# Gated linear attention into a mixture of experts: row products over 128 rows of the array, empty rows written later, eight unread products fewer

## The chip, the cores and the metric

The kernel runs on one core of a Trainium2 chip. A core has engines that run side by side and meet only at semaphores: TensorE (PE in the profile; its weight loads are PEld), VectorE (DVE), ScalarE (ACT), GpSimd (POOL) and SyncE (SP), which here issues most of the transfers. TensorE multiplies out of on-chip memory (SBUF) into eight accumulation banks (PSUM). The metric is the device time of one execution in microseconds; the median of several runs is compared.

## The reference

Inputs q, k, v and a complex gate a are 4 batches x 8 heads x 768 steps x 48 channels, f32. First a gated recurrence runs over the steps of each head; then every token (3072 of them, 384 channels) goes to the one of eight experts with the highest logit:

```python
scale = np.minimum(mag, 0.999) / (mag + 1e-06)
for t in range(S):
    new_re = ar * S_re - ai * S_im
    new_im = ar * S_im + ai * S_re
    S_re, S_im = (new_re + kv, new_im)
    y[:, :, t] = np.einsum('bhd,bhde->bhe', q[:, :, t], S_re)
...
logits = x @ w_gate + modality_bias[modality_id]
e_idx = np.argmax(logits, axis=1)
h = np.maximum(x[mask] @ w1[e], 0.0)
out[mask] = gate_w[mask, None] * (h @ w2[e])
```

## The kernel before

The sequence is cut into 6 chunks of 128 steps; a chunk of one batch is a **unit**, so there are 24 units, taken in pairs (groups). Within a chunk the recurrence is written as a masked product. Logarithms of the moduli and turns of the phases are summed over the steps by TensorE (`sums`, L240; `angles`, L194), and ScalarE makes exponentials, sines and cosines of them. `hats` multiplies these into q and k (L276, L280). `turned` transposes the result (L304) with 64 rows of the array at a time. `inner` makes the masked weights (`wp`, L321) and the update of the state (`up`, L329). `outer` makes the unit's output y, transposed (`yp`, L353 and L359), in a tile whose partitions 0 to 63 and 64 to 127 hold an even and an odd head, 48 channels and 16 of zeros each; ScalarE copies it to `yT` (L360).

`rows` (L363) then turns y back into rows of tokens and makes the logits in the same products: the moving operand `sel` has an identity of 48 columns and the 48 x 8 gate weights behind it. One product per head: 4 pairs x 2 halves, each with 64 rows of the array and 56 columns, the two halves into two PSUM banks. ScalarE copies the 384 channels to bf16 (L381), and VectorE adds the eight partial logits per expert (L382).

The **router** (`take`, called after units 7, 15, 19 and 23) adds the bias, finds the best expert, ranks the tokens of each expert with small products (`rank`), and GpSimd scatters the rows to their expert's region in device memory (`x_rows`, L657). Unused places there are filled from two columns of 128 empty rows that the router's constructor writes once (L540). The constructor is called at the end of loop turn 0 and also loads the modality bias and the modality of each token (L555, L557), from which VectorE makes the bias of each token (L573 to L577).

The **expert layers** gather 256 rows at a time, transpose them (L922), multiply by w1 (L940), apply the ReLU, multiply by w2 (L955), scale by the gate weight (L958) and scatter to the output (L960).

`dense(to, n)` (L88) issues n products whose result nobody reads; they lie ahead of the transposes of certain units (`FILLED`, by unit number) and ahead of the `rank` products from unit 16 on (four, and none at the last take). Each carries an order edge to lie behind the last products traced before.

The loop at L434 traces one turn per unit, with every stage at its own offset: in turn w come the loads, `turned` of unit w+2, `sums` (even turns), `inner` of w+1, `outer` of w, `rows` of w-1, `angles` (odd turns to 15). The order in which each engine gets its instructions isn't that of the text throughout: a planner sets it at build time, from priorities, its own costs of instructions, and the times at which it expects operands, except where order edges or a hand-written stretch (the late expert layers) fix it. On each engine the order is then strict. The transfers of SP's queue also go out in that order, and one that waits holds up those behind it.

Of the kernel before, what the change touches and what calls it, by code (L numbers as in the profile page):

```python
# [11 lines left out]
F32 = mybir.dt.float32  # L12
BF16 = mybir.dt.bfloat16
AX = mybir.AxisListType
Alu = mybir.AluOpType
# [8 lines left out]
def gate_loop(nc, ctx, tc, cpool, ident, q, k, v, a_re, a_im, sel, lg, make_router, make_layers):  # L24
# [4 lines left out]
    B, H, S, D = q.shape  # L29
    L = 128  # L30
    G = S // L
    J = H // 2
    C = 2 * D
# [32 lines left out]
    box = {}  # L66
# [28 lines left out]
            if i == 0 and busy:  # L95
                tc.add_manual_dep(ins.ins, busy[-1].ins.name, mybir.DependencyInfo(mybir.DependencyClass.NoSync, mybir.DependencyReason.DATA), reason="behind the products before it")

    FILLED = {2: 10, 3: 5, 4: 5, 5: 5, 15: 4}

    abs_ = io.tile([L, 2, 2, NG, H, D], F32, name="abs", bufs=1)  # L100
    css = el.tile([L, 2, NG, H, 2, D], F32, name="css", bufs=1)
# [261 lines left out]
    def rows(g, b):  # L363

        yT = box.pop(("outer", g, b))
        xw = pair([L, J, D + Router.E], "xw")
        for j in range(J):
            for u in range(2):
                at_u = slice(u * 64, (u + 1) * 64)
                ins = nc.tensor.matmul(xw[:, u, j], yT[at_u, j], sel[at_u, j], start=True, stop=True)  # L370
        busy.append(ins)
        m = g * B + b
        m0 = max(c for c in takes.values() if c <= m)
        if m == m0:
            n = min([c for c in takes.values() if c > m] + [NU]) - m
            packed = un.tile([L, 8, Router.W], U32, name="packed")
            nc.gpsimd.iota(packed[:, 0:n, Router.W - 1].rearrange("p (g b) -> p g b", b=B), pattern=[[L, n // B], [S, B]], base=g * L, channel_multiplier=1)
            box["packed"] = packed
        packed = box["packed"]
        xr = packed[:, m - m0, 0:H * D // 2].bitcast(BF16)  # L380
        nc.scalar.copy(xr.rearrange("t (j u d) -> t u j d", u=2, d=D), xw[:, :, :, 0:D])  # L381
        nc.vector.tensor_reduce(lg[:, m, :], xw[:, :, :, D:].rearrange("t u j e -> t e u j"), axis=AX.XY, op=Alu.add)  # L382

    NX = len(groups)
    NU = len(order)
# [1 line left out]
    late = []  # L387
    EARLY = Router.EARLY
    takes = {7: 0, EARLY - 1: 8, 19: EARLY, NU - 1: 20}
# [42 lines left out]
    rt = None  # L432
    open_ = []
    for w in range(-4, NU + 1):  # L434


        even = w % 2 == 0
        x = w // 2

        n = w + 1 if w < 0 else w  # L440
        unit(values, n + 2)
        unit(values, n + 3)
        if even:
            phase(load_a, x + 6)
            phase(carries, x + 4)
            phase(fractions, x + 3)
        else:
            phase(load_qk, x + 3)
            phase(decays, x + 2)
            hats(n + 3)  # L450
            if w == -3:
                hats(0)
        unit(turned, n + 2)
        if even:
            if x + 2 < NX:
                table(EXP)
            phase(sums, x + 2)
            phase(moduli, x + 2)
            phase(logs, x + 4)
        elif x + 3 < NX:  # L460
            table(TRIG)
            phase(arctans, x + 4)
        unit(inner, n + 1)
        if even:
            for f in late:
                f(act)
            late.clear()
        unit(outer, n)
        if even:
            hats(n + 3)  # L470
            phase(tangents, x + 4)
        else:
            phase(waves, x + 3)
            phase(squares, x + 5)
            phase(products, x + 5)
        if w == NU:
            layers.turn(0)
        unit(rows, n - 1)
        if not even:
            phase(angles, x + 4)  # L480
        if w == 0:
            rt = make_router(ctx, ps, bank)
        open_ = [t for t in open_ if next(t, True) is None]
        if w - 1 in takes:
            open_.append(rt.take(takes[w - 1], w, late, box["packed"], lambda n: dense(box["full"][:, 0], n)))
            next(open_[-1])
        if w == 15:
            layers = make_layers(rt, io, el, un, bank, pair, abs_, css)
        if w > 15:
            layers.before(w, box)  # L490
# [5 lines left out]
class Router:  # L496
# [20 lines left out]
    def __init__(self, nc, ctx, tc, keep, ps, bank, lg, x_rows, moe_modality_id, moe_modality_bias, N, Dt, E, B, G):  # L517
# [19 lines left out]
        nc.gpsimd.memset(empty[:, 0:self.W - 1], 0)  # L537
        nc.gpsimd.memset(empty[:, self.W - 1:], self.FAR)
        self.blank = x_rows[E * self.S:E * self.S + 2 * TP, :]
        nc.sync.dma_start(out=self.blank[None], in_=empty[:, None, :].broadcast_to([1, 2 * TP, self.W]))  # L540
        self.expert = keep.tile([1, self.NE + self.NR + self.NSMALL + 1], I32, name="expert")
        self.column = keep.tile([1, self.NE + self.NR + self.NSMALL + 1], I32, name="column")
        self.SURE = self.NBIG + 1
# [41 lines left out]
            self.tc.declare_no_dep(put.ins, group="first loads", reason="the first tiles hold tokens of the first columns alone")  # L585
            self.tc.add_to_no_dep_group("late rows", put.ins)

    def take(self, m0, m1, late, packed, dense):

        nc, rp, TP, E = self.nc, self.rp, self.TP, self.E  # L590
        n = m1 - m0
        last = m1 == len(self.tile_of)
        M = 8

        def t(name, shape, dt=F32):
            full = rp.tile([TP, M] + shape, dt, name=name)
            return full[:, 0:n]

        def bc(ap):
            return ap[:, :, None].broadcast_to([TP, n, E])  # L600

        l = t("l", [E])
        nc.vector.tensor_tensor(l, self.lg[:, m0:m1], self.bias[:, m0:m1], Alu.add)
        mx = t("mx", [])
        nc.vector.tensor_reduce(mx, l, axis=AX.X, op=Alu.max)
        sh = t("sh", [E])
        nc.vector.tensor_tensor(sh, l, bc(mx), Alu.subtract)

        cand = t("cand", [E])
        nc.vector.scalar_tensor_tensor(cand, sh, 0.0, self.pref[:, None, :].broadcast_to([TP, n, E]), Alu.is_ge, Alu.mult)  # L610
        best = t("best", [])
        nc.vector.tensor_reduce(best, cand, axis=AX.X, op=Alu.max)
        oneh = t("oneh", [E], BF16)
        nc.vector.tensor_tensor(oneh, cand, bc(best), Alu.is_equal)
        before = self.acc
        acc = rp.tile([TP, E], BF16, name="acc", bufs=4)
        with nc.allow_low_precision("counts of at most 24"):
            nc.vector.tensor_reduce(acc[:], oneh.rearrange("p i e -> p e i"), axis=AX.X, op=Alu.add)
        if before is not None:
            nc.vector.tensor_tensor(acc[:], acc[:], before, Alu.add)  # L620
        self.acc = acc[:]

        def weights(act):
            ex = t("ex", [E])
            act(ex, sh, Act.Exp)
            sm = t("sm", [])
            nc.vector.tensor_reduce(sm, ex, axis=AX.X, op=Alu.add)
            nc.vector.reciprocal(packed[:, 0:n, self.W - 2].bitcast(F32), sm)

        late.append(weights)  # L630
        yield

        rank = self.bank([TP, M, E], "rank")
        if m0 >= self.EARLY:
            dense(0 if last else 4)
        nc.tensor.matmul(rank[:, 0:n], self.tri[:], oneh, start=True, stop=False)
        if before is not None:
            nc.tensor.matmul(rank[:, 0:n], self.ones[:], before[:, None, :].broadcast_to([TP, n, E]), start=False, stop=False)
        for i in range(n - 1):
            nc.tensor.matmul(rank[:, i + 1:n], self.ones[:], oneh[:, i:i + 1, :].broadcast_to([TP, n - 1 - i, E]), start=False, stop=i == n - 2)  # L640
        own = t("own", [E])
        nc.vector.tensor_tensor(own, rank[:, 0:n], oneh, Alu.mult)
        pos = t("pos", [])
        nc.vector.tensor_reduce(pos, own, axis=AX.X, op=Alu.add)
        nc.vector.scalar_tensor_tensor(pos, best, -float(self.S), pos, Alu.mult, Alu.add)
        place = t("place", [], U32)
        nc.vector.tensor_scalar(place, pos, float(E * self.S), None, Alu.add)
        if m0 == 0:
            self.guess()
        if m1 == self.EARLY:  # L650
            self.early_places()
        if not last:
            yield
        for i in range(n):
            if i == 4:
                yield
            put = self.put = nc.gpsimd.indirect_dma_start(out=self.x_rows, out_offset=bass.IndirectOffsetOnAxis(ap=place[:, i:i + 1], axis=0), in_=packed[:, i], in_offset=None, bounds_check=E * self.S - 1, oob_is_err=False)  # L657
            self.put_row(put, m0 >= self.EARLY)
        if m0 == self.EARLY:
            self.tc.add_manual_dep(nc.gpsimd.drain().ins, put.ins.name, mybir.DependencyInfo(mybir.DependencyClass.NoSync, mybir.DependencyReason.DATA), reason="the queue's list is cleared behind these")  # L660
        if last:
            self.places()
# [341 lines left out]
def kernel(  # L1004
# [27 lines left out]
    nc.vector.tensor_copy(identb[:], ident[:])  # L1032
    lg = cpool.tile([128, N // 128, E], F32, name="lg")

    sel = cpool.tile([128, H // 2, D + E], F32, name="sel")
    nc.gpsimd.memset(sel[:], 0.0)
    for u in range(2):
        nc.gpsimd.tensor_copy(sel[u * 64:u * 64 + D, :, 0:D], ident[u * 64:u * 64 + D, None, u * 64:u * 64 + D].broadcast_to([D, H // 2, D]))
        nc.sync.dma_start(out=sel[u * 64:u * 64 + D, :, D:], in_=moe_w_gate.rearrange("(j u d) e -> u d j e", u=2, d=D)[u])

    last, layers = gate_loop(
        nc, ctx, tc, cpool, ident, q, k, v, a_re, a_im, sel, lg,
# [33 lines left out]
```

## Time and profile before

| | us |
|---|---|
| median of three runs | 333.67 (334.74, 333.67, 328.97) |
| the profiled execution | 329.75 |
| its span in the profile | 328.1 |
| TensorE products / weight loads busy | 294.4 / 227.9 |
| VectorE busy | 242.2 |
| ScalarE busy | 240.5 |
| GpSimd busy | 70.2 |

The mean clock that TensorE was granted over the span is 0.969 of full speed. A row of instructions in order of time has its start, its length, the engine, the source line, the operation, the tiles (written<-read), the shapes (for a product rows*columns of the loaded operand and rows x columns of the moving one) and how many are merged; in brackets stand the engine's idle time before it and what ended that. A group's row has busy time and mean length in ns of one after the bar. Idle time of an engine that others don't wait for costs nothing.

### The profile page before, as it was taken

The page shows a single profiled execution, that of the slowest core. Times are in us where ns is not written, and L with a number is a line of the kernel's source. Part 1 is how long each engine was busy: PE and PEld are TensorE (multiplying, and loading weights), DVE is VectorE, ACT ScalarE, POOL GpSimd, SP SyncE. Part 2 cuts the span into 40 slices and gives each one's busy share as a digit, 9 for nine tenths or more (in the row PEclk, how much of TensorE's full clock was granted, in tenths as well). Part 3 has the DMA queues.
Part 4 walks back from the last instruction along what each step waited for, and adds up shares of the span by engine and source line. Part 5 has one row for each costly group of instructions (what it writes and reads, how often), then busy time and mean ns, then how long its engine had stood idle before and what let it go on. Part 6 is the DMA issues. An engine that isn't in the chain of part 4 may idle for free.

```text
span 328.1 us, 11561 instructions
## 1 busy us (share of the span) xinstructions
PE 294.4 (90%) x4950; PEld 227.9 (69%) x4950; DVE 242.2 (74%) x443; ACT 240.5 (73%) x289; POOL 70.2 (21%) x91
## 2 busy tenths in 40 slices
PE   1797899899499899989999999999998999999991
PEld 0343566658378686867778877889987677777770
DVE  1749699994679999999899987995436944555530
ACT  3889699999559899988999997655324666554541
POOL 8000000000000000001872000018541564332423
PEclk9899799979969999999999999999999999999998
DMA  7967897789884978676558977211591564332211
GB/s 135 208 139 147 168 193 125 114 79 176 177 170 89 160 168 154 140 142 135 132 118 141 190 131 147 51 28 54 100 231 59 152 212 147 98 119 97 100 62 57
DMA packets 155282, 43.04 MB, mean 131 GB/s; under 512 B 145602, under 2 KB 151494, under 8 KB 155096
## 3 DMA queue, kind: packets, MB, share of 16 engines
q1 hardware_dynamic: 149592, 31.98, 50.7%
q0 software_dynamic: 5632, 10.25, 11.7%
q8 instruction: 41, 0.67, 0.8%
q14 instruction: 17, 0.14, 0.1%
HBM read 38.00 MB, written 9.15 MB: 144 GB/s over the span
## 4 chain that ended last, share of the span: by engine, by line
PE 48%; ACT 26%; DVE 13%; issue 5%; DMA 4%; SPq 2%; POOL 1%; POOLq 0%; DVEq 0%; ACTq 0%
PE h_ps L940 9%; PE y_ps L955 9%; ACT sq L119 5%; ACT L116 5%; PE up L329 5%; PE xw L370 4%; PE ls L240 4%; PE yp L359 3%; ACT css L119 3%; ACT pm L119 3%; PE wp L321 3%; PE u L194 3%; PE yp L353 2%; DVE QK L280 2%; ACT KT L305 2%
## 5 line engine op out<-in xcount | busy, mean ns | idle before, releaser
L657 POOL DMA_INDIRECT x_rows<-packed,place x24 | 34.5, 1436 | 208.1 <-DVE lm L175 146.7
L280 DVE TENSOR_TENSOR QK<-css,qkp 128x1536 f32<-128x1536 f32 x24 | 42.0, 1751 | 0.1
L329 PE MATMUL up<-V,QK 64*96 64x48 f32 x704 | 37.5, 247 | 0.9 <-DVE lg L382 0.8
L329 PEld LDWEIGHTS up<-V,QK 64*96 64x96 f32 x704 | 34.5, 161 | 2.8 <-DVE lg L382 1.0
L955 PE MATMUL y_ps<-w2t,hT 128*128 128x384 bf16 x200 | 34.7, 326 | 0.7 <-ACT hT L943 0.7
L940 PE MATMUL h_ps<-xgT,w1t 128*128 128x256 bf16 (+1 forms) x312 | 34.9, 268 | 0.0
L116 ACT ACT_TABLE_LOAD x25 | 32.1, 1283 | 1.4 <-PEq L1060 0.9
L960 POOL DMA_INDIRECT out_dram<-y_sb,xg x25 | 25.4, 1014 | 35.8 <-ACT y_sb L958 31.5
L940 PEld LDWEIGHTS <-w1t 128*128 128x128 bf16 x312 | 29.5, 98 | 4.6
L305 ACT COPY KT<-tKT 96x1024 f32<-96x1024 f32 x24 | 24.2, 1008 | 9.0 <-PE tKT L304 8.8
L321 PEld LDWEIGHTS wp<-QT,KT 96*64 96x64 f32 x768 | 24.7, 139 | 8.6 <-ACT yT L360 2.8
L321 PE MATMUL wp<-QT,KT 96*64 96x64 f32 x768 | 28.0, 226 | 1.9 <-ACT yT L360 1.8
L958 ACT ACTIVATE y_sb<-y_ps,xg 128x384 f32<-128x384 f32 x25 | 13.2, 578 | 22.3 <-PE y_ps L955 18.2
L360 ACT COPY yT<-yp 128x512 f32<-128x512 f32 x24 | 14.0, 584 | 20.5 <-PE yp L359 20.3
L955 PEld LDWEIGHTS <-hT 128*128 128x128 bf16 x200 | 18.9, 98 | 12.5 <-issue 0.5
L370 PE MATMUL xw<-sel,yT 64*128 64x56 f32 x384 | 26.4, 277 | 0.6 <-ACT QT L305 0.6
L370 PEld LDWEIGHTS xw<-sel,yT 64*128 64x128 f32 x384 | 23.3, 187 | 2.6 <-ACT QT L305 0.7
L305 ACT COPY QT<-tQT 96x1024 f32<-96x1024 f32 x24 | 24.3, 1014 | 0.0
L119 ACT ACTIVATE sq<-sq 128x1536 f32<-128x1536 f32 (+1 forms) x20 | 23.3, 1165 | 1.4 <-DVE sq L150 1.2
L304 PEld LDWEIGHTS tKT<-ident,QK 64*96 64x96 f32 x384 | 13.2, 129 | 14.1 <-issue 8.2
L945 DVE TENSOR_SCALAR hT<-h_ps 128x1024 bf16<-128x1024 f32 (+1 forms) x9 | 10.5, 1166 | 16.8 <-PE h_ps L940 16.8
L119 ACT ACTIVATE pm<-ls 128x768 f32<-128x768 f32 x24 | 18.2, 809 | 6.5 <-PE ls L241 6.4
(197 smaller groups left out, 590.9 us busy)
## 6 DMA issues: line engine op xcount, KB each, us to landing
abs<-in_a_re_dram SPq DMA_DIRECT2D x24, 192.0 KB, 3.7
abs<-in_a_im_dram SPq DMA_DIRECT2D x24, 192.0 KB, 3.8
qk<-in_q_dram SPq DMA_DIRECT2D x24, 192.0 KB, 3.8
qk<-in_k_dram SPq DMA_DIRECT2D x24, 192.0 KB, 3.8
V<-in_v_dram SPq DMA_DIRECT2D x24, 192.0 KB, 3.7
cb<-f_scr SPq DMA_DIRECT2D x10, 384.0 KB, 4.6
xg<-x_rows SPq DMA_DIRECT2D x12, 194.0 KB, 2.4
x_rows<-x_rows SPq DMA_DIRECT2D x8, 194.0 KB, 3.3
```

Source lines behind the costliest of these rows:

```text
L116: then(nc.scalar.preload_act_table_set(name))
L119: then(nc.scalar.activation(*args, **kw))
L280: nc.vector.tensor_tensor(QK[:].rearrange("p a h c d -> p a (h c d)"), wave, twice, Alu.mult)
L305: nc.scalar.copy(to[:], tp)
L321: nc.tensor.matmul(wp[rows_, h, :], KT[:, s, h], QT[:, s, h], start=True, stop=True)
L329: ins = nc.tensor.matmul(up[:, s, h], flat[rows_, h * C:(h + 1) * C], V[rows_, h, 0:D], start=True, stop=True)
L360: nc.scalar.copy(yT[:].rearrange("p j (s t) -> p s j t", s=2), yps)
L370: ins = nc.tensor.matmul(xw[:, u, j], yT[at_u, j], sel[at_u, j], start=True, stop=True)
L657: put = self.put = nc.gpsimd.indirect_dma_start(out=self.x_rows, out_offset=bass.IndirectOffsetOnAxis(ap=place[:, i:i + 1], axis=0), in_=p ...
L940: nc.tensor.matmul(h_ps[:, f // nf, f % nf, :], w1t[:, k, ff * 128:(ff + 1) * 128], xgT[:, k, :], start=(k == 0), stop=(k == KD - 1))
L955: nc.tensor.matmul(y_both[:, s], self.hT[:, f, s * 128:(s + 1) * 128], w2t[:, f, :], start=(f == 0), stop=(f == NF - 1))
L960: sc = self.sc = nc.gpsimd.indirect_dma_start(out=self.out, out_offset=bass.IndirectOffsetOnAxis(ap=xg[:, Dt // 2 + 1:], axis=0), in_=y_sb ...
```

## The change

Three things change. The row products of a unit become four, each over all 128 rows of the array: `sel` now holds, for each pair of heads, the identity of the even head in columns 0 to 47 of its rows, that of the odd head in columns 48 to 95, zeros elsewhere, and the gate weights in the eight columns behind, so that a product has 104 columns and adds both heads' logits itself. They go into one PSUM bank. ScalarE copies the same 384 channels from it; VectorE adds four partial logits per expert, not eight. The empty rows are written when the first routing step is traced (after turn 8's other work), not in the constructor. And eight unread products go: four ahead of unit 15's transposes, four ahead of the `rank` products of units 16 to 19.

```diff
-    FILLED = {2: 10, 3: 5, 4: 5, 5: 5, 15: 4}
+    FILLED = {2: 10, 3: 5, 4: 5, 5: 5}
...
-        xw = pair([L, J, D + Router.E], "xw")
+        xw = bank([L, J, C + Router.E], "xw")
         for j in range(J):
-            for u in range(2):
-                at_u = slice(u * 64, (u + 1) * 64)
-                ins = nc.tensor.matmul(xw[:, u, j], yT[at_u, j], sel[at_u, j], start=True, stop=True)
+            ins = nc.tensor.matmul(xw[:, j], yT[:, j], sel[:, j], start=True, stop=True)
...
-        nc.scalar.copy(xr.rearrange("t (j u d) -> t u j d", u=2, d=D), xw[:, :, :, 0:D])
-        nc.vector.tensor_reduce(lg[:, m, :], xw[:, :, :, D:].rearrange("t u j e -> t e u j"), axis=AX.XY, op=Alu.add)
+        nc.scalar.copy(xr.rearrange("t (j c) -> t j c", c=C), xw[:, :, 0:C])
+        nc.vector.tensor_reduce(lg[:, m, :], xw[:, :, C:].rearrange("t j e -> t e j"), axis=AX.X, op=Alu.add)
...
-        nc.sync.dma_start(out=self.blank[None], in_=empty[:, None, :].broadcast_to([1, 2 * TP, self.W]))
+        self.empty = empty
...
+        if m0 == 0:
+            nc.sync.dma_start(out=self.blank[None], in_=self.empty[:, None, :].broadcast_to([1, 2 * TP, self.W]))
...
-        if m0 >= self.EARLY:
-            dense(0 if last else 4)
...
-    sel = cpool.tile([128, H // 2, D + E], F32, name="sel")
+    sel = cpool.tile([128, H // 2, 2 * D + E], F32, name="sel")
     nc.gpsimd.memset(sel[:], 0.0)
     for u in range(2):
-        nc.gpsimd.tensor_copy(sel[u * 64:u * 64 + D, :, 0:D], ident[u * 64:u * 64 + D, None, u * 64:u * 64 + D].broadcast_to([D, H // 2, D]))
-        nc.sync.dma_start(out=sel[u * 64:u * 64 + D, :, D:], in_=moe_w_gate.rearrange("(j u d) e -> u d j e", u=2, d=D)[u])
+        nc.gpsimd.tensor_copy(sel[u * 64:u * 64 + D, :, u * D:(u + 1) * D], ident[u * 64:u * 64 + D, None, u * 64:u * 64 + D].broadcast_to([D, H // 2, D]))
+        nc.sync.dma_start(out=sel[u * 64:u * 64 + D, :, 2 * D:], in_=moe_w_gate.rearrange("(j u d) e -> u d j e", u=2, d=D)[u])
```

More of the change, by code (lines that the diff above doesn't have):

```diff
@@ L484, in gate_loop @@
         if w - 1 in takes:
-            open_.append(rt.take(takes[w - 1], w, late, box["packed"], lambda n: dense(box["full"][:, 0], n)))
+            open_.append(rt.take(takes[w - 1], w, late, box["packed"]))
             next(open_[-1])
@@ L586, in put_row, with take @@
             self.tc.add_to_no_dep_group("late rows", put.ins)
-    def take(self, m0, m1, late, packed, dense):
+    def take(self, m0, m1, late, packed):
         nc, rp, TP, E = self.nc, self.rp, self.TP, self.E
```

## The prediction

> **What bounds the kernel now.** I read the page's shares first, then the chain that ended last, then stretches of 5 us.
>
> ```profile
> span 328.1 us, 11561 instructions
> PE 294.4 (90%) x4950; PEld 227.9 (69%) x4950; DVE 242.2 (74%) x443; ACT 240.5 (73%) x289; POOL 70.2 (21%) x91
> PE 48%; ACT 26%; DVE 13%; issue 5%; DMA 4%; SPq 2%; POOL 1%; POOLq 0%; DVEq 0%; ACTq 0%
> ```
>
> PE (TensorE) holds half of the chain and ACT (ScalarE) a quarter, so no one engine bounds all of it. Columns of the next rows: stretch; length; busy time (count) of PE, PEld, DVE, ACT, POOL; granted clock; DMA share; GB/s.
>
> ```profile
> 75.00:80.00 5.00, 5.00 (x123) 3.94 (x116) 2.80 (x6) 4.94 (x8) 0.00 (x0) 1.00 1.00 164
> 90.00:95.00 5.00, 4.88 (x37) 3.22 (x38) 4.91 (x7) 1.92 (x2) 0.00 (x0) 0.50 1.09 209
> 165.00:170.00 5.00, 5.00 (x131) 4.20 (x131) 4.93 (x8) 4.64 (x6) 4.09 (x4) 1.00 0.27 77
> 230.00:235.00 5.00, 5.00 (x151) 4.72 (x149) 1.61 (x7) 2.31 (x5) 3.33 (x5) 1.00 0.29 67
> ```
>
> Three things are to be seen. Up to about 85 us ACT has no gap, and PE is filled up with unread products. At 90 to 95 us PE works at half clock, behind a gap that is shown with the rivals. From about 157 us on PE is full at clock 1.00; at 165 DVE (VectorE) and ACT are nearly full too, at 230 PE alone is. So PE time saved counts from 157 on, wholly after 205; before that it meets ACT.
>
> **The row products.** The rows are of two units, one followed by transposes of 64 rows (L304), one by a product of 128 rows (L194), and of a pair of 128-row f32 products (L240) with its loads.
>
> ```profile
> 187.56 1.10 PE L370 MATMUL xw<-sel,yT 64*128 64x56 f32 x16
> 188.50 0.61 PE L304 MATMUL tKT<-ident,QK 64*96 64x64 f32 x16
> 187.56 0.97 PEld L370 LDWEIGHTS xw<-sel,yT 64*128 64x128 f32 x16
> 188.39 0.57 PEld L304 LDWEIGHTS tKT<-ident,QK 64*96 64x96 f32 x16
> 194.83 1.10 PE L370 MATMUL xw<-sel,yT 64*128 64x56 f32 x16
> 195.86 0.91 PE L194 MATMUL u<-tan,turn 128*128 128x384 f32 x2
> 181.36 0.91 PE L240 MATMUL ls<-lm,half 128*128 128x384 f32 x2
> 182.11 0.33 PE L241 MATMUL ls<-off,nhalfb 128*128 128x384 bf16 x1
> 182.27 0.81 PE L240 MATMUL ls<-lm,half 128*128 128x384 f32 x2
> 182.92 0.33 PE L241 MATMUL ls<-off,nhalfb 128*128 128x384 bf16 x1
> 181.36 0.30 PEld L240 LDWEIGHTS ls<-lm,half 128*128 128x128 f32 x2
> L370 PEld LDWEIGHTS xw<-sel,yT 64*128 64x128 f32 x384 | 23.3, 187 | 2.6 <-ACT QT L305 0.7
> ```
>
> The code issues 8 f32 products a unit and the trace has 16 records, two for each, so four products will leave 8. What does one cost? The second L240 pair takes 182.92 - 182.27 = 0.65 us: 0.325 each for 384 columns, 0.85 ns a column, the load hidden. The first pair, whose first load lies open, takes 182.11 - 181.36 = 0.75, so a load of 128 f32 columns occupies the array for 0.10. Now: 16 loads run 0.97 from first start to last end; less the last one's 0.19 the sixteenth starts 0.78 after the first, 0.052 apart. That is 0.10 for each pair: the two halves of the array load side by side. After: eight full loads, one behind another, 0.10 each, and under each a stream of 104 columns, 104 x 0.85 = 0.09, which is shorter. So 8 x 0.10 + 0.09 = 0.89 us of array time, against 8 x 0.10 + 56 x 0.85 = 0.85 now. **Halving the count removes no load time.**
>
> What differs is the neighbour. Now transposes behind the row products load at 188.39 - 187.56 = 0.83, a 128-row product only at 195.86 - 194.83 = 1.03, its own load (0.10) in the open. After, a 128-row product can load during the last stream: it streams at about 0.95 instead of 1.13, **-0.18**. Transposes come behind a change of row size, which the second pair of rows prices at about 0.1 over the work: they load at 1.0 instead of 0.83, **+0.17**. From 157 us on stand units 10 to 23; by the code's order seven have 128-row followers (fillers taken out), six have transposes, one neither: -1.26 + 1.02 = -0.2. Before 157 us ACT's chain covers either; without that cover the ten units there, half of each kind, would change it by no more than 0.2.
>
> The Trainium skill, "TensorE: Matmul & The Clock Gate", section "Part 3: Packing small matmuls — row/col tiling", says that weight loads overlap running products only when their row groups differ. By that rule the eight full loads would stand in series with their products, and the change would be slow; it is the second rival below. The trace disagrees in its nearest rows: the second L240 pair (0.65) shows no load time, with all 128 rows in use.
>
> **The unread products.** Their place in the chain (start, length):
>
> ```profile
> 171.30 0.97 PE tKT L92 x4
> ...
> 239.36 0.97 PE rank L92 x4
> 181.03 1.01 ACT L305 COPY KT<-tKT 96x1024 f32<-96x1024 f32 x1 [0.32 <-PE tKT L304]
> 183.28 1.51 ACT L119 ACTIVATE pm<-ls 128x768 f32<-128x768 f32 x2 [0.33 <-PE ls L241]
> 247.22 0.33 PE L353 MATMUL yp<-W,V 64*64 64x64 f32 x3 [0.92 <-issue]
> ```
>
> Eight go, 0.97 us per four, both in the chain. With the first four gone, ACT is late next: it waits 0.32 + 0.33 = 0.65 us for PE and then carries the chain itself for some us, so **-0.65**. The second four lie where PE alone is full: **-0.9**, the little left being the rank products' load. Bounds: the issue stall of 0.92 at 247 may swallow it (0), or all counts (-0.97). PE stays full on both sides of either place, so I see no clock loss.
>
> **Readers of the products, and the empty rows.**
>
> ```profile
> L381 ACT CAST packed<-xw 128x384 bf16<-128x384 f32 x24 | 11.6, 482 | 3.1 <-PE xw L370 3.1
> L382 DVE TENSOR_REDUCE lg<-xw 128x8 f32<-128x64 f32 x24 | 5.3, 220 | 13.8 <-ACT packed L381 13.8
> L605 DVE TENSOR_REDUCE mx<-l 128x8 f32<-128x64 f32 x2 | 0.4, 214 | 0.0
> L605 DVE TENSOR_REDUCE mx<-l 128x4 f32<-128x32 f32 x2 | 0.4, 186 | 0.1
> 60.53 0.65 SPq L540 DMA_DIRECT2D x_rows<-empty  x1
> 61.87 7.87 SPq L557 DMA_DIRECT2D mid<-in_moe_modality_id_dram  x4
> 132.81 0.24 SPq L253 DMA_DIRECT2D m_scr<-pm  x1
> 139.04 0.53 SPq L285 DMA_DIRECT2D V<-in_v_dram  x1
> 142.58 0.39 SPq L131 DMA_DIRECT2D abs<-in_a_re_dram  x1
> L657 POOL DMA_INDIRECT x_rows<-packed,place x24: 967/1044/4507, 154.5 to 261.2; - x24
> ```
>
> ACT copies the same 384 elements: 0. The reduce reads 32 elements, not 64: 28 ns by the L605 rows, 0.7 us over 24, of which DVE's 13% of the chain makes **-0.1**. The wider table takes gpsimd at most as long again to clear, during the first load: 0.
>
> The empty rows' transfer leaves SP at 60.53 and returns about 133 us, behind the stores of the first routing turn and ahead of that turn's V, q and k loads. It frees 0.65 us of issue ahead of the slow mid loads, but no engine waits for a transfer there: 0, at best -0.65. At the new place the loads behind it come 0.65 later; they are used a turn or more on, and SP is idle from 139.57 to 142.58, which takes it up: 0, at worst +0.65. The scatters of rows into the same tensor may now have to wait for it; the first is issued at 154.5, and cover of over 10 us is left.
>
> Sum: -0.65 - 0.9 - 0.2 - 0.1 = **-1.85 us**, against the profiled execution's 329.75 us (span 328.1 and 1.65 around it). That execution lies 3.9 under the median; the three runs and it have a mean of 331.8. I take that: **330 us**.
>
> **Rivals.** The order on each engine comes from a planner that weighs its own costs and arrival times, and three of its inputs change: the products, the fillers, SP's queue. What that may touch is this gap:
>
> ```profile
> 84.53 0.96 DVE L150 TENSOR_TENSOR sq<-sq 128x768 f32<-128x768 f32 x1 [3.55 <-ACT sq L119]
> 85.41 0.17 DVE L573 TENSOR_SCALAR is_m<-mid 128x24 f32<-128x24 int32 x1
> 86.62 0.36 DVE L577 TENSOR_TENSOR bias<-bias,bias_m 128x192 f32<-128x192 f32 x1
> 88.23 1.75 DVE L280 TENSOR_TENSOR QK<-css,qkp 128x1536 f32<-128x1536 f32 x1
> 90.12 1.09 PE L304 MATMUL tKT<-ident,QK 64*96 64x64 f32 x16 [4.33 <-DVE QK L280]
> 95.49 1.48 PE L321 MATMUL wp<-QT,KT 96*64 96x64 f32 x32
> ```
>
> *The gap shrinks.* DVE stands 3.55 us before sq, then does five bias operations (1.5 us, 85.41 to 86.9) while PE waits for QK. They read mid, which is issued behind the empty rows now. If the planner sees mid earlier and puts them ahead of sq, they fit into DVE's idle time: -1.5. If PE then keeps its clock, half of the 5.4 us from 90.12 to 95.49 goes too: -2.7. From 331.8 with the sum and these: 328.4 or 325.7; if the whole 4.33 and the slow clock go, 323. For it: the order of the first operations depends on just this queue. Against it: 0.65 us is little.
>
> *Loads in series.* Eight records at 0.10 + 0.09 make 1.5 us, +0.5 a unit, +7 over the fourteen units from 157 us on, +12 over all; with the fillers' gain 337 to 343. It decides from 0.13 us a record on. For it stands the rule named above; against it the L240 pair. This one ends slower.
>
> *A new gap.* The same replanning puts an operation that waits ahead of a QK, where now none does; one such place costs what this one does, 4.3 idle and 2.7 at half clock: 331.8 + 7.0 - 1.85 = 337, from the median 333.67 without the gain 341. For it: DVE has 4.9 busy us of 5 in the stretches at 90 and at 165, so a QK put late has no slack to catch up in.
>
> *No effect*: ACT covers the first fillers and the issue stall the second: 331.8 to 333.7.
>
> **How the numbers follow.** Forecast 330 (326.5 to 334): 0.43. Gap shrinks: 0.23. Loads in series: 0.13. New gap: 0.14. No effect: 0.07. Measurement tells about 2% of 333.67, so 327.0 and 340.3 are the borders. Below: most of the shrinking gap (0.18) and the forecast's edge (0.07): 0.25. Above: two thirds of the two slow cases: 0.18. Within: 0.57. Range 323.5 to 342.
>
> **What would show it.** Row products: 8 records a unit, 128x104, loads 0.10 apart, the next L194 load 0.8 behind the first. If they are 0.19 apart the series rival holds. The L92 group has four records fewer under tKT and none under rank; KT and pm at about 181 to 183 no longer wait for PE. The empty rows stand on SP at about 133 us, the V load behind them has no reader waiting. The bias operations' place on DVE and the clock at 90 to 95 tell whether the gap moved. I am wrong if PE takes over 1.2 us a unit for row products, or if any engine's order before 160 us differs and opens or closes a gap of over 2 us.

## The result, and the profile after

The changed kernel takes 332.53 us (median of 20 executions, 329.03 to 341.26), the kernel before beside it 330.24 (20 executions, 327.6 to 338.29). The ratio is **1.0067, interval 1.0038 to 1.0096**: slower by some 2 us, where the forecast had a gain of 1.85. Some executions of any kernel here run some per cent longer at a lower granted clock, and all ratios are taken without them. The profiled execution after has 332.50 us, its span is 330.9.

The page after: span, the engines' shares, and the shares of the chain that ended last.

```profile
span 330.9 us, 11159 instructions
PE 295.2 (89%) x4750; PEld 229.1 (69%) x4750; DVE 241.4 (73%) x443; ACT 240.3 (73%) x289; POOL 71.6 (22%) x91
PE 41%; ACT 21%; DVE 16%; DMA 8%; issue 7%; SPq 3%; POOL 2%; POOLq 0%; DVEq 0%; ACTq 0%
```

400 instructions and 200 products fewer, and PE still busy 0.8 us longer: part of its work ran at a lower clock. The chain has less PE and ACT, more DVE, and DMA and issue have grown. To see where the time went, follow one mark through both timelines, the start of each unit's row products (us):

| unit | before | after | difference |
|---|---|---|---|
| 0 | 62.5 | 63.5 | +1.0 |
| 3 | 100.0 | 93.6 | -6.4 |
| 7 | 134.3 | 128.0 | -6.3 |
| 8 | 141.4 | 139.3 | -2.1 |
| 10 | 160.3 | 158.0 | -2.3 |
| 11 | 170.2 | 173.7 | +3.5 |
| 23 | 250.0 | 251.7 | +1.7 |
| end of the last product | 321.9 | 324.6 | +2.7 |

So the change first wins 6.4 us over the kernel before, where the gap of PE at 86 to 90 us has gone, loses 4.2 of it at unit 8 and 5.8 more at unit 11, wins 1.8 by unit 23 and loses 1.0 behind it, in the expert layers. The two losses are new gaps of PE. The timeline of PE and DVE after, at both (start, length; in brackets the idle time ahead and what ended it):

```profile
134.35 0.26 PE L359 MATMUL yp<-QT,state 96*48 96x64 f32 x1
137.44 0.99 PE L359 MATMUL yp<-QT,state 96*48 96x64 f32 x14 [2.83 <-issue]
...
159.61 0.96 DVE L150 TENSOR_TENSOR sq<-sq 128x768 f32<-128x768 f32 x1 [3.95 <-ACT sq L119]
160.48 0.95 DVE L276 TENSOR_TENSOR qkp<-qk,pm 128x768 f32<-128x768 f32 x1
161.81 1.75 DVE L280 TENSOR_TENSOR QK<-css,qkp 128x1536 f32<-128x1536 f32 x1
163.71 1.09 PE L304 MATMUL tKT<-ident,QK 64*96 64x64 f32 x16 [2.94 <-DVE QK L280]
```

In the first, PE stops in the middle of one run of products and waits for no semaphore ("issue"). In the second it waits for a QK that stands on DVE behind sq, and sq waits 3.95 us for ACT: the picture of the old gap, 75 us later. Behind each gap the granted clock falls (stretches of 5 us; after the five engines come clock, DMA share, GB/s):

```profile
135.00:140.00 5.00, 2.56 (x34) 2.42 (x35) 3.55 (x10) 2.68 (x3) 0.00 (x0) 0.58 0.99 193
165.00:170.00 5.00, 5.00 (x37) 2.82 (x35) 3.47 (x5) 2.57 (x4) 4.39 (x3) 0.50 0.42 106
```

What stands just ahead of the first gap is the part that was priced at nothing. SP's queue after (the empty rows and the loads behind them):

```profile
126.34 0.64 SPq L601 DMA_DIRECT2D x_rows<-empty  x1
...
127.68 5.08 SPq L138 DMA_DIRECT2D qk<-in_q_dram  x1
132.80 2.68 SPq L139 DMA_DIRECT2D qk<-in_k_dram  x1
```

SP is done with the empty rows after 0.64 us, but a q load behind them takes 5.08 to issue; the other q loads take 0.4 to 2.3 us, most of them under 1. The stretches of 1 us of the same kernel tell why:

```profile
127.00:128.00 1.00, 1.00 (x36) 0.92 (x33) 1.00 (x2) 1.00 (x2) 0.00 (x0) 1.00 0.20 13
...
133.00:134.00 1.00, 1.00 (x36) 0.95 (x36) 1.00 (x3) 1.00 (x2) 0.00 (x0) 1.00 0.77 26
135.00:136.00 1.00, 0.00 (x0) 0.00 (x0) 1.00 (x3) 0.98 (x2) 0.00 (x0) 0.92 1.23 253
```

The engines of the transfers are about 0.8 busy for 7 us and move 26 GB/s; at 135, when that is over, they move 253. The 256 pieces of 776 bytes take 0.36 us each and are under way from 127.63 to 135.20 us: **198,656 bytes in 7.57 us, 26 GB/s, all out of one partition**. In the kernel before the same pieces stood at 61.82 to 69.36, ahead of the loads of mid. The queues after, in the stretch 127 to 135 us and from 135 to 137.5:

```profile
q1 hardware_dynamic: 471, 0.24, 69.8%
...
q8 instruction: 1, 0.02, 2.2%
```

Packets of the instruction queue (16 KB each) have come every 5 to 11 us up to here, the last one at 125.62; none comes from 127 to 135, the next starts at 135.13, and PE goes on at 137.44. That the missing instructions were PE's is inferred from the order of these times; the runs below test it.

The row products themselves look as the prediction drew them: two units after, one ahead of 128-row products, one ahead of transposes.

```profile
180.16 1.14 PE L368 MATMUL xw<-sel,yT 128*128 128x104 f32 x8
181.13 0.83 PE L194 MATMUL u<-tan,turn 128*128 128x384 f32 x2
191.14 1.14 PE L368 MATMUL xw<-sel,yT 128*128 128x104 f32 x8
192.21 0.65 PE L304 MATMUL tKT<-ident,QK 64*96 64x64 f32 x16
180.16 0.97 PEld L368 LDWEIGHTS xw<-sel,yT 128*128 128x128 f32 x8
181.04 0.30 PEld L194 LDWEIGHTS u<-tan,turn 128*128 128x128 f32 x2
L380 DVE TENSOR_REDUCE lg<-xw 128x8 f32<-128x32 f32 x24 | 4.5, 187 | 14.3 <-ACT packed L379 14.3
```

### The profile page after: what moved, and what is told of

Its sections match the earlier page's. It is cut to its first block, busy times and chain, and to the rows that moved or that the text cites. A ratio compares the mean times of both kernels' runs of the same rounds, so it can differ in the third digit from the quotient of the medians.

```text
span 330.9 us, 11159 instructions
## 1 busy us (share of the span) xinstructions
PE 295.2 (89%) x4750; PEld 229.1 (69%) x4750; DVE 241.4 (73%) x443; ACT 240.3 (73%) x289; POOL 71.6 (22%) x91
## 4 chain that ended last, share of the span: by engine, by line
PE 41%; ACT 21%; DVE 16%; DMA 8%; issue 7%; SPq 3%; POOL 2%; POOLq 0%; DVEq 0%; ACTq 0%
PE h_ps L938 6%; PE y_ps L953 6%; PE up L329 5%; ACT css L119 4%; PE xw L368 4%; PE ls L240 4%; ACT sq L119 4%; PE yp L359 3%; ACT L116 3%; PE wp L321 3%; DMA abs<-in_a_im_dram 3%; DVE QK L280 3%; PE u L194 3%; ACT pm L119 3%; DVE qkp L276 2%
## 5 line engine op out<-in xcount | busy, mean ns | idle before, releaser
L655 POOL DMA_INDIRECT x_rows<-packed,place x24 | 35.2, 1466 | 57.5 <-DVE U L339 38.1
L854 POOL DMA_DIRECT2D abs<-in_moe_w_dram x2 | 1.8, 902 | 152.5 <-ACT sq L119 151.4
L368 PE MATMUL xw<-sel,yT 128*128 128x104 f32 x192 | 28.2, 291 | 0.5 <-ACT QT L305 0.5
L368 PEld LDWEIGHTS xw<-sel,yT 128*128 128x128 f32 x192 | 24.0, 197 | 2.4 <-ACT QT L305 0.6
L194 PE MATMUL u<-tan,turn 128*128 128x384 f32 x48 | 23.1, 568 | 2.8 <-ACT tan L119 2.1
L240 PE MATMUL ls<-lm,half 128*128 128x384 f32 x48 | 21.8, 539 | 1.5 <-DVE lg L380 1.0
```

The lines of the kernel that those rows point to most:

```text
L194: nc.tensor.matmul(us[:, i], turn[:], tan[:, i], start=True, stop=False)
L240: nc.tensor.matmul(ls[:, i], half[:], lm[:, i], start=True, stop=False)
L368: ins = nc.tensor.matmul(xw[:, j], yT[:, j], sel[:, j], start=True, stop=True)
```

## The experiments

The theory: the slow transfer out of one partition makes the loss, in two ways, by holding all transfer engines (PE's instructions come late) and by setting the planner's order (hats stand late). Rivals: the products or the fillers cost what was not seen; or the place of the transfer matters, not its length. Runs sent together share a chip and the kernel before. On two of the four chips used, every kernel took some 10% longer than on the others (the kernel before 365 to 368 us, against 332 to 333), so only ratios are compared, and those of one chip first.

### Each part alone

The three parts, each put alone into the kernel before: the row products with their readers and `sel`; the two lines of the empty rows; the fillers of unit 15 and of `rank`.

```diff
-                ins = nc.tensor.matmul(xw[:, u, j], yT[at_u, j], sel[at_u, j], start=True, stop=True)
+            ins = nc.tensor.matmul(xw[:, j], yT[:, j], sel[:, j], start=True, stop=True)
```

```diff
-        nc.sync.dma_start(out=self.blank[None], in_=empty[:, None, :].broadcast_to([1, 2 * TP, self.W]))
+        self.empty = empty
...
+        if m0 == 0:
+            nc.sync.dma_start(out=self.blank[None], in_=self.empty[:, None, :].broadcast_to([1, 2 * TP, self.W]))
```

```diff
-    FILLED = {2: 10, 3: 5, 4: 5, 5: 5, 15: 4}
+    FILLED = {2: 10, 3: 5, 4: 5, 5: 5}
...
-            dense(0 if last else 4)
```

> Only the row products change (eight records of 128 rows and 104 columns a unit); empty rows and unread products stay as before. Theory A (the empty rows' transfer and the order that the planner makes around it carry the change): within 0.3% of before, since eight full loads of 0.10 us take what sixteen half loads took in pairs; 1.07 us a unit ahead of transposes, 0.9 ahead of a 128-row product. Rival B (the row products carry it): 0.5 to 1% slower, the whole of the measured difference.

> Only the empty rows move to the first routing step. Theory A: 0.5 to 1.2% slower than before, somewhat more than the whole change, since the unread products are still there; the transfer (256 packets of one row each out of one partition, 0.36 us a packet) holds the transfer engines for about 7.5 us at its new place, PE stands 2 to 3 us there for its next instructions and then has half clock for 6.8 us; VectorE's order differs from before as in the changed kernel, and the gap at 86 us is gone. Rival B: within 0.3% of before.

> Only the eight unread products go. Both theories: 0.3 to 0.5% faster (0.65 and 0.9 us by the prediction), all orders as before. If they hold up the clock, or ScalarE takes the place: 0 to 0.5% slower.

Measured: row products **0.9927** (0.9886 to 0.9967), a gain of 2.4 us; fillers out **1.0041** (0.9998 to 1.0085), no gain; the empty rows gave no ratio in this run (median 334.3 of 6, beside 332.18), so they ran again:

> The move of the empty rows alone, with the slow transfer, nothing else changed: the part of the change that was priced at nothing. Theory (it takes the gap at 86 us away, and sets PE's stall and VectorE's late hats behind the transfer's new place): ratio 1.0 to 1.015, so with the row products (0.9927 alone) it makes up the kernel after. Rival (the move is neutral or gains, and the loss comes of the parts together): 0.985 to 0.998.

Measured, on one of the slower chips: **1.0125** (1.0049 to 1.0201). The product of the three ratios is 1.009, the whole change 1.0067: within the noise the parts make up the result, and the move of the empty rows is what turned it. In its trace the old gap is gone and the new one is there, with the old row products and all fillers:

```profile
160.71 1.09 PE L304 MATMUL tKT<-ident,QK 64*96 64x64 f32 x16 [2.80 <-DVE QK L280]
```

The stall of PE at 135 us, which both expectations had foreseen, is in neither trace of this kernel, and it isn't in the kernel before, where no packet of instructions came between 60.21 and 70.97 us either and PE didn't stop for one. Why some kernels with the slow transfer have the stall and others not is left open. So the move alone loses in another way than the whole change. In the first of its two traces unit 8's row products start 7.3 us earlier than in the kernel before, unit 11's 0.2 later and unit 12's 2.5 later: all of the loss lies behind the one new gap, here with 17.07 us of half clock from 158.5 us on. The traced executions took 334.89 and 369.05 us, those behind the 1.0125 361.9 to 362.7, so how the 1.0125 is made up isn't shown.

### Another source, the same bytes

The kernel after, with the empty rows read from 128 partitions, two rows from each:

```diff
-        empty = rc.tile([1, self.W], U32, name="empty")
+        empty = rc.tile([TP, 2, self.W], U32, name="empty")
...
-            nc.sync.dma_start(out=self.blank[None], in_=self.empty[:, None, :].broadcast_to([1, 2 * TP, self.W]))
+            nc.sync.dma_start(out=self.blank.rearrange("(p c) w -> p c w", c=2), in_=self.empty[:])
```

> The changed kernel with one edit: the empty rows lie in 128 partitions, two in each, and go out as 128 pieces of 1552 bytes, at the same place of SP's queue. Theory A: the transfer takes 1 to 2 us instead of 7.5, SP's next q load no 5 us, PE's stall of 2.8 us for instructions at about 134 us goes and with it the half clock: 3 to 6 us less than the changed kernel, so 0.3 to 1.2% faster than before. Rival (the stall for instructions has nothing to do with the transfer): the stall stays, 0.5 to 0.8% slower than before.

> The same kernel as the run with the empty rows out of 128 partitions at the new place (ratio 0.9665 there), beside the two above on one chip. Theory: 0.955 to 0.975; both gaps gone, transfer under 1.5 us.

Measured: **0.9665** (0.9565 to 0.9765), and on another chip **0.9752** (0.9681 to 0.9823). SP's queue and two stretches of the first:

```profile
126.58 0.37 SPq L601 DMA_DIRECT2D x_rows<-empty  x1
...
127.92 0.57 SPq L138 DMA_DIRECT2D qk<-in_q_dram  x1
...
135.00:140.00 5.00, 4.40 (x67) 3.29 (x63) 5.00 (x17) 3.67 (x5) 0.00 (x0) 1.00 0.80 157
165.00:170.00 5.00, 4.05 (x124) 3.64 (x121) 4.97 (x6) 4.99 (x8) 0.97 (x2) 1.00 0.90 108
```

The q load behind the empty rows issues in 0.57, both gaps and both stretches of low clock are gone. The gain is larger than expected, since the expectation had counted PE's stall alone. The order on PE is that of the kernel after; on DVE 35 of 443 places hold another operation, and sq stands behind the QK that it had held up. Unit 8's row products start 3.7 us earlier than after (135.6, not 139.3), unit 11's 10.2 (163.5, not 173.7), the last one's 10.3. So the two gaps cost about 4 and 6 us, and both go with the slow transfer: the stall with PE's order unchanged, the second gap with a new order on DVE. The packets of instructions say more of the stall: here one starts at 126.53 and the next at 131.37, where the kernel after, with the same order on PE, has none from 125.62 to 135.13. A packet was due, by this, while the slow transfer held the engines.

Is it the number of the transfer's pieces or the one partition that makes it slow? Two more kernels keep the order on PE, DVE and ACT row for row as after: the same bytes in half as many pieces out of the one partition, and the same pieces out of two.

```diff
-        empty = rc.tile([1, self.W], U32, name="empty")
+        empty = rc.tile([1, 2, self.W], U32, name="empty")
...
+            nc.sync.dma_start(out=self.blank.rearrange("(p c) w -> p (c w)", c=2)[None], in_=self.empty.rearrange("o c w -> o (c w)")[:, None, :].broadcast_to([1, TP, 2 * self.W]))
```

> The kernel after, and the same 194 KB from the same one partition, but as 128 pieces of two rows (1552 bytes) in place of 256 of one (776 bytes). The order on TensorE, VectorE and ScalarE is that of the kernel after, so only the transfer can differ. Theory (a partition gives some 26 GB/s whatever the pieces): the transfer still holds the engines about 7.5 us, the stall of PE behind it stays at 2.5 to 3 us, the gap at VectorE's late hats stays, ratio within 0.005 of that of the kernel after (1.0067). Rival (each piece has a price of its own, about 0.03 us of the whole): the transfer takes 3.5 to 4 us, the stall shrinks to below 1 us, ratio 0.99 to 1.0.

```diff
-        empty = rc.tile([1, self.W], U32, name="empty")
+        empty = rc.tile([2, self.W], U32, name="empty")
...
+            nc.sync.dma_start(out=self.blank.rearrange("(p c) w -> p c w", c=128), in_=self.empty[:, None, :].broadcast_to([2, 128, self.W]))
```

> The kernel after, and the same 256 pieces of 776 bytes, from two partitions (128 from each). The order on TensorE, VectorE and ScalarE is that of the kernel after. Theory (the rate is that of a partition): the transfer takes 3.5 to 4 us, PE's stall behind it shrinks to below 1.5 us and, where it falls under some 2 us, the half clock behind it goes; the gap at the late hats stays, as the order does: ratio 0.985 to 1.0. Rival (the rate is that of the pieces): 7.5 us and the stall as in the kernel after, ratio 1.0 to 1.01.

Half as many pieces: ratio 1.0028 (0.997 to 1.0087). A piece takes 0.80 us, not 0.36, and the whole 7.4 us, as before: it is **the bytes out of the one partition**, not the number of pieces, that count. The stall is there too. A stretch of 4 us within the transfer, and the stall's row:

```profile
126.00:130.00 4.00, 3.82 (x96) 3.43 (x90) 4.00 (x7) 3.97 (x6) 0.00 (x0) 1.00 0.85 28
136.01 0.99 PE L359 MATMUL yp<-QT,state 96*48 96x64 f32 x14 [2.80 <-issue]
```

Two partitions: ratio 0.979 (0.9704 to 0.9876). The stall at 135 is gone, but not as expected. The transfer did not get shorter, it got longer: 126.4 to 135.8 us, each piece 0.067 us. A stretch within it, the instruction queue in 126 to 135.6 us, SP's queue, and the gap of the order in this kernel:

```profile
127.00:128.00 1.00, 1.00 (x19) 0.90 (x19) 1.00 (x3) 0.99 (x2) 0.00 (x0) 1.00 0.11 20
q8 instruction: 2, 0.03, 1.6%
128.62 4.60 SPq L138 DMA_DIRECT2D qk<-in_q_dram  x1
157.25 0.92 PE L304 MATMUL tKT<-ident,QK 64*96 64x64 f32 x16 [2.94 <-DVE QK L280]
```

The DMA share in that stretch is 0.11, about 2 of 16: 256 pieces of 0.067 are 17.2 us of work, 8.6 on each of two engines. The loads on SP are still held up (4.60), but two packets of instructions get through (128.79 and 133.25), and PE doesn't stop at 135. So what counts for the stall, as far as this pair shows, is **how many engines are held at once**, not how long the transfer lasts. Holding all sixteen isn't enough by itself: the kernel before and the move alone held them for 7.5 us and had no stall. The Trainium skill, "DMA: Bandwidth & Descriptors", section "Why a DMA increments its semaphore by 16 and not by 1", says that the number of engines of a transfer is the largest one up to 16 that divides the slowest dimension above 1 on both of its sides, which is 256 in the kernel after and 2 in this one; this trace agrees (share 0.11 beside 0.8). Partitions and engines both changed here, so what two partitions give with sixteen engines isn't shown. The gap at the late hats, 2.94 after and 2.94 here, stays with the order. And an "issue" stall needs no slow transfer: the same trace, of an execution of 331.83 us, has one much later, with 13.65 us of half clock about it, while the transfers move 226 GB/s (238 to 241 us).

```profile
240.86 0.48 PE L353 MATMUL yp<-W,V 64*64 64x64 f32 x3 [2.52 <-issue]
```

The second gap by itself: the kernel after, slow transfer and all, with one order edge that keeps sq behind the hats traced before it (in the traces sq and one qkp stand elsewhere on DVE, eight places in all):

```diff
+        if "hat" in box:
+            tc.add_manual_dep(add.ins, box["hat"].ins.name, mybir.DependencyInfo(mybir.DependencyClass.NoSync, mybir.DependencyReason.DATA), reason="behind the hats traced before it")
...
-        nc.vector.tensor_tensor(QK[:].rearrange("p a h c d -> p a (h c d)"), wave, twice, Alu.mult)
+        box["hat"] = nc.vector.tensor_tensor(QK[:].rearrange("p a h c d -> p a (h c d)"), wave, twice, Alu.mult)
```

> The kernel after with the slow transfer as it is, and one order edge on VectorE: the sum of squares (L150) may not stand ahead of the hats traced before it. Only four places on VectorE differ. It separates the two new gaps of PE: the one at 160.8 to 163.7 us is a matter of order and goes (2.9 us and some 3 us of the half clock behind it), the one at 134.6 to 137.4 us is the wait behind the slow transfer and stays. Theory: 1 to 2 per cent faster than the kernel after, ratio to before 0.985 to 0.997. Rival (the gap at 161 is only where an earlier delay comes out; closed there it opens at the next hats): ratio 1.003 to 1.01, with another gap of over 2 us between 150 and 180 us.

Measured: 0.9896 (0.9809 to 0.9983), on one of the slower chips. Its rows at the two places:

```profile
136.35 0.98 PE L361 MATMUL yp<-QT,state 96*48 96x64 f32 x14 [2.88 <-issue]
161.17 0.65 PE L306 MATMUL tKT<-ident,QK 64*96 64x64 f32 x16 [0.76 <-ACT yT L362]
```

The stall stays at 2.88, the gap shrinks from 2.94 to 0.76. The two are separate, as the theory says; against 1.0067 the order alone is worth about 1.7%, though that compares two chips.

### Place, and the unread products

The fast transfer at its old place: in the kernel before otherwise unchanged; with row products and fillers out; with row products alone.

```diff
-        nc.sync.dma_start(out=self.blank[None], in_=empty[:, None, :].broadcast_to([1, 2 * TP, self.W]))
+        nc.sync.dma_start(out=self.blank.rearrange("(p c) w -> p c w", c=2), in_=empty[:])
```

> The kernel before; of the empty rows only the source is another: 128 partitions x 2 rows of SBUF in place of one partition read 256 times. Place, products and fillers stay. Theory (it is the slow transfer out of one partition that costs, wherever it stands): the stretch of 25 to 30 GB/s at 61.5 to 69 us goes, the mid and V loads behind it leave about 6 us earlier (V at 63 to 65 us, not 69.8), VectorE's bias operations find their operands earlier, and the gap of PE at 85.8 to 90.1 shrinks or goes: 324 to 329 us against 332 of the kernel before, ratio 0.975 to 0.99. Rival (the place decides, since whatever stands in SP's queue there moves the planner's order): gap at 86 stays at 4 us or more, ratio 0.995 to 1.005.

> The kernel after, with the empty rows' transfer out of 128 partitions, and at its old place in the router's constructor. Beside the run with that transfer at the new place (ratio 0.9665) it tells whether the place matters once the transfer is short. Theory (only its length matters): ratio 0.96 to 0.975. Rival (the move itself gives most of the gain, by taking the transfer from ahead of the mid loads): ratio 0.985 to 1.0, with PE's gap at 86 us open again.

> Row products over 128 rows, the unread products kept, and the empty rows out of 128 partitions at their old place, in the router's constructor; it differs from the one above by the place alone. Theory (only the transfer's length matters): within 0.005 of the one above, PE's gap at 86 us gone here too. Rival (the place matters of itself): 0.01 or more slower.

Measured: **0.9821** (0.9735 to 0.9908), 0.9687 (0.9588 to 0.9787) and 0.9669 (0.958 to 0.9757). In the first, mid leaves in 2.39 us in place of 7.87, V at 64.28 in place of 69.78, and the old gap is closed:

```profile
85.00:90.00 5.00, 4.92 (x75) 3.05 (x73) 4.11 (x8) 4.58 (x7) 0.00 (x0) 1.00 0.86 162
```

The last is to be read beside the next three runs, which keep or drop the eight unread products at the new place with the fast transfer.

> Row products over 128 rows and the empty rows at the new place out of 128 partitions, with the eight unread products kept. Beside the same without them (ratio 0.9665) it prices the unread products where no slow transfer disturbs. Forecast's step (-0.65 and -0.9 us of 324): ratio 0.970 to 0.972. Rival (they are covered by ScalarE and by a fetch stall, and worth nothing): ratio 0.9645 to 0.9685.

> The same kernel as the run with row products, the empty rows out of 128 partitions at the new place, and the unread products kept (0.9606 on another chip), now beside the one without them on one chip. Forecast's step (-0.65 and -0.9 us): slower than that one by 0.003 to 0.006 of the time. Rival (the unread products are worth nothing, or keep the clock up): equal within 0.002, or faster.

> Once more the kernel after with the empty rows out of 128 partitions (0.9665 and 0.9752 so far), beside the next one on one chip, with more executions. If the removed unread products are worth what was forecast, this is 0.003 to 0.006 faster than the next; if their removal costs, as the two earlier pairs hint (0.008 and 0.009), it is slower by that.

> Once more row products and the empty rows out of 128 partitions at the new place, with the unread products kept (0.9606 and 0.9659 so far). Forecast's step: 0.003 to 0.006 slower than the one above. Hint of the earlier pairs: 0.008 faster.

Kept: 0.9606 (0.9537 to 0.9674), **0.9659** (0.9602 to 0.9716), 0.9655 (0.9585 to 0.9724). At the old place 0.9669 against the last of these on the same chip: no effect of the place is seen once the transfer is short. Dropped, on the same chips: 0.9687 (at the old place), 0.9752, and no ratio in the third (six executions of 347.1 to 362.1, median 354.7; the kept one's median is 345.4). In both pairs with ratios the kernel that keeps the products is the faster one, by 0.8% and 0.9%, but the intervals overlap, and the first pair differs in the place too. So no gain of dropping them is seen, and a loss isn't shown. The traces on one chip show why nothing is gained. Dropped, from one unit's row products to the next:

```profile
163.71 1.14 PE L368 MATMUL xw<-sel,yT 128*128 128x104 f32 x8
164.78 0.65 PE L304 MATMUL tKT<-ident,QK 64*96 64x64 f32 x16
166.06 1.15 PE L321 MATMUL wp<-QT,KT 96*64 96x64 f32 x32 [0.18 <-ACT yT L360]
167.98 1.56 PE L329 MATMUL up<-V,QK 64*96 64x48 f32 x32 [0.77 <-DVE lg L380]
171.12 1.14 PE L368 MATMUL xw<-sel,yT 128*128 128x104 f32 x8
236.04 0.33 PE L353 MATMUL yp<-W,V 64*64 64x64 f32 x3 [0.34 <-issue]
```

Kept:

```profile
165.00 1.14 PE L368 MATMUL xw<-sel,yT 128*128 128x104 f32 x8
165.97 1.03 PE L92 MATMUL tKT<-halfb 128*128 128x512 bf16 x4
169.27 1.56 PE L329 MATMUL up<-V,QK 64*96 64x48 f32 x32 [0.15 <-DVE lg L380]
172.41 1.14 PE L368 MATMUL xw<-sel,yT 128*128 128x104 f32 x8
```

Both take 7.41 us from row products to row products: without the four, PE waits 0.18 for ACT and 0.77 for DVE's lg instead. At the second place 6.04 us in place of 6.26 remain, the rest lies in a fetch stall. Whether the kernel that keeps them is really *faster* isn't settled, nor why it would be: these two traces, whose orders before 160 us differ much, show no single place for 2 us.

The best version is row products, empty rows from 128 partitions, unread products kept: some 3.5% faster than the kernel before.

## Why the prediction was wrong, point by point

**The step that failed** is the term of the empty rows: "It frees 0.65 us of issue ahead of the slow mid loads, but no engine waits for a transfer there: 0, at best -0.65", and "at worst +0.65" at the new place. 0.65 us is SP's issue; the transfer holds sixteen engines for 7.5. The prediction quoted the row that shows it, four mid loads of 6 KB in 7.87 us, called them slow and didn't ask what made them so. The page of the kernel before has its GB/s in 40 slices of 8.2 us, and the ninth, from 65.6 us on, falls to 79:

```profile
GB/s 135 208 139 147 168 193 125 114 79 176 177 170 89 160 168 154 140 142 135 132 118 141 190 131 147 51 28 54 100 231 59 152 212 147 98 119 97 100 62 57
```

Its size was to be had: the Trainium skill, "SBUF — State Buffer", section "Door 1: The DMA port swizzle", gives a transfer 27.2 GB/s for each port that its partitions reach, and one partition reaches one; the traces show 26. An estimate from that figure is 198,656 / 27.2 = 7.3 us.

Both rivals that were drawn from this queue came true at once, and 7.5 in place of 0.65 would have spoken for both. *The gap shrinks* (0.23): "for it: the order of the first operations depends on just this queue"; mid is issued in 3.08 us, not 7.87, the bias operations move up from 85.41 to 70.16, the whole gap goes, worth 6.4 us at unit 3 (the prediction had put 4.3 and 2.7 on it in case all of it went). "Against it: 0.65 us is little" was the same wrong size. The row of mid after:

```profile
62.00 3.08 SPq L555 DMA_DIRECT2D mid<-in_moe_modality_id_dram  x4
```

*A new gap* (0.14): an operation that waits, sq again, came ahead of a QK, worth 5.8 us where the rival had 7.0. The prediction treated the two as exclusive, at prices of opposite sign; they are one cause, moved from 62 to 127 us, and nearly cancel. What no rival had is the third effect, PE's stall behind its own instructions, 4.2 us. The three together: -6.4 + 4.2 + 5.8, some 3.6 us; with the 1.8 won by unit 23 and the 1.0 lost behind it, that is the table's 2.7 within 0.1. The move alone measured nearly the same (1.0125, 4.1 us of 330), but its traces have no stall, so that is not this sum confirmed. That the time came out so near to the forecast 330 us is luck: a gain of 6.4 and losses of 10.0, none of them in the sum, nearly cancelled.

**Row products: right in kind, wrong in sum.** 8 records, 104 columns; the next L194 load starts 0.88 behind the first load (0.8 forecast), and the rival *Loads in series* (1.5 us a unit) is refuted. The neighbours came out at 0.97 for 1.03 (-0.06, not -0.18) ahead of 128-row products and at 1.07 for 0.94 (+0.13, forecast +0.17) ahead of transposes: by the same count of units +0.4, not -0.2. Yet the part alone gained 2.4. PE's waits before and, in the second fence, with the row products alone (total, times, longest):

```profile
PE wp L321 <- ACT yT L360: 1.8, 5, 0.4
PE yp L353 <- issue: 1.5, 2, 0.9
PE ls L240 <- DVE lg L382: 0.8, 1, 0.8
```

```profile
PE wp L321 <- ACT yT L360: 0.9, 4, 0.2
PE yp L359 <- issue: 0.5, 1, 0.5
```

1.0 us of fetch stalls, 0.8 of a wait for the logits and 0.9 of one for yT are gone, 2.7 in all, against 0.4 of array time; the span is 2.0 shorter. What PE waits longer for is mostly ACT's off (2.3 to 3.4), ahead of 20 us, and there it costs nothing: unit 0's row products start 0.2 earlier than in the kernel before. The prediction counted array time and the reduce (220 to 187 ns, 33 less where 28 was forecast) and not what 192 fewer products, and as many fewer loads, take off the instruction stream. That the stalls left because the stream is shorter is argued, not tested by itself, and each side of this comparison is one trace.

**Unread products:** -0.65 and -0.9 forecast, 0 and at most -0.2 in the traces. The first was limited by ACT in the forecast; DVE's lg, late in the same place, takes the rest. At the second, the bound that was named ("the issue stall of 0.92 at 247 may swallow it") is what happened: with the fillers alone taken out, the stall at 246 was 1.40.

**The clock:** "PE stays full on both sides of either place, so I see no clock loss" holds for the fillers; the loss came behind the two new gaps.

## What to carry to other kernels

A transfer is priced by what it holds, not by its issue: look at the issue length of the load *behind* it and at GB/s beside the DMA share, and read a constant that goes to many rows from many partitions. When a cheap-looking step moves, follow its whole shadow to the new place, and where a planner sets the order, expect the gap that it caused to move with it rather than to vanish. Work taken off one engine counts only if no other engine's result is due at the same point: put the next releaser's lateness beside the time saved before it enters the sum.

## What the runs showed of the hardware that had not been expected

- One partition as the source gives 26 GB/s over sixteen engines: 7.57 us for 256 pieces of 776 bytes, 7.4 us for 128 of 1552. With two engines at work a piece of 776 bytes took 0.067 us, not 0.36; from 128 partitions the whole was under way for 0.9 us (127.69 to 128.58).
- A transfer with two in its outermost dimension ran on about two engines (share 0.11): it took longer (9.4 us), and PE had no stall behind it.
- PE's instructions come, as far as the order of times can show, by the same engines: with all of them held, no packet of instructions for 8 us and a stall of 2.8 to 2.9 in three kernels; with two held, no stall there. In two other kernels all were held as long and PE didn't stop.
- In the kernel after, the idle gaps of 2.83 and 2.94 us each had 6.83 us at half clock, which begin within the gap; such a gap cost 4 to 6 us in all by the table of units. In other traces the half clock about a gap of 2.5 to 2.9 lasted from 3.41 to 17.07 us.
